# Odd planes of an inverse transform loaded in two parts, skipped columns, merged edge matmuls and one empty slot

## The chip, the cores and the metric

The kernel runs on one core of a Trainium2 chip. The metric is the device time of one execution in microseconds (us). The core has TensorE (PE: matmuls, and PEld: its weight loads), VectorE (DVE), ScalarE (ACT), GpSimd (POOL) and SyncE (SP), which here only issues DMAs. All DMAs run on the same 16 DMA engines. DRAM is the memory off the core, SBUF the memory on it (128 partitions), PSUM the buffer that matmuls write.

## The reference

For x of 2048 rows (s) and 1024 columns (d), with xn = layernorm(x) over d:

```python
X = rfft2(xn)                  # over s and d: 2048 x 513, complex
s = irfft2(X * (w_r + 1j * w_i))
h = silu(xn @ w1)              # w1: 1024 x 3584
g = silu(h @ w2)               # w2: 3584 x 1024
return x + s * g
```

Inputs and output are float32. Each float32 factor of a large product is split into a high and a low float16 part, and three matmuls (high by high, high by low, low by high) stand for one.

## The kernel before, in words

**Stages.** The kernel runs two lines of work side by side. The large one is the feed-forward part: xn @ w1 (mm1, line 491), then h @ w2 (mm2, line 580). The second product uses a scheme of seven products m (PRODUCTS, line 39), each with eight row blocks j. One (m, j) has two halves k of 21 matmuls, so there are 112 halves; half 2n + k is that of block n = 8m + j. The hidden layer lies in DRAM and comes back in ht tiles (load_h, line 558), two per block, from seven buffers; the w2 tiles are split into high and low by a generator (w2_gen, line 438) that takes one step per work call: it issues the load of a raw tile jr four steps ahead, and for products 4 and 5 a second load w, which GpSimd adds to jr (line 457) before ScalarE (high, line 284) and VectorE (low, line 287) split it.

The small line of work is the transform: a forward transform over d and s, a multiplication by the filter, and the inverse over s and then over d. Its matmuls stand between the halves of the large product.

**Planes.** f_gen (line 1029) makes the filtered spectrum in 16 steps u = 4q + j. The results of one q are four planes c of 1024 float16 columns in a high and a low part, stored to DRAM tiles zd[c] (lines 1099 to 1104). Planes 0 and 2 are one DMA per q. Planes 1 and 3 are two, one for each half r of the columns. edge_gen (line 1204) makes a correction for the first column of each group from nine small float32 matmuls (lines 1231 to 1233), which reverse the partition order with a permutation matrix.

**Inverse.** i_gen(c) (line 1324) handles one plane; the order is 1, 3, 0, 2 (IORDER). load_i(c) loads the plane into zt and its cosine table into kk, each in one buffer. For odd c it issues four DMAs of 512 KB, each to 64 partitions (first or second half r, row parity e), 8 KB in each partition, and then kk. edge_in (line 1315) copies the correction into zt. Then come four batches g: mat(g) is 24 matmuls of the inverse over s (line 1350 for odd c, 1358 for even), post(g) the butterflies on ScalarE and VectorE, split(g) the halves us for the next matmuls (lines 1428 and 1429). mat2(p), four times, is the inverse over d: 24 matmuls (line 1439) that read all four us tiles, and bfly(p) its butterflies.

**What sets the order.** Each engine runs its own instructions in the order in which the program issues them. The two lines of work are Python generators: after each half of mm2, tick() runs the issues that were deferred by a count of ticks (defer, line 203) and are due, and work() (line 1601) then takes steps of the transform's queue bg, at most three, until one yields PAUSE or until the planned clock of VectorE is more than LEAD = 1.0 us ahead of that of TensorE, and then one step of w2_gen. The planned clocks add costs by size (lines 241 to 252): 0.085 us + 1.045 ns per element and partition on VectorE, 0.4215 ns per column on TensorE; VectorE's clock is held at no more than 1 us behind TensorE's. switch() (line 1558) opens the pool of the inverse and calls load_i(1), and takes five more steps with PAUSE before i_gen(1) begins. close() runs all deferred issues. In this phase load_i(1) is called behind half 44, mat(0) of plane 1 behind half 50, and mat2(0) behind half 58; load_i(3) behind half 57.

Of the kernel before, what the change touches and what calls it, by code (L numbers as in the profile page):

```python
# [10 lines left out]
F16 = mybir.dt.float16  # L11
# [15 lines left out]
LEAD, PAUSE, LAST = 1.0, -1, 6  # L27
SECOND = 0.085, 1.045e-3
IORDER = (1, 3, 0, 2)
# [124 lines left out]
def spectral_ffn(ctx, tc, x, w_r, w_i, w1, w2, ca, kc, ci, tw, pm, out):  # L154
    nc = tc.nc
# [6 lines left out]
    ki = [kc[c][:, 1024:3088] for c in range(4)]  # L162
    wv = [t.rearrange("(m2 m1 q) k -> q m1 m2 k", m2=4, q=4) for t in (w_r, w_i)]

    dp = ctx.enter_context(tc.tile_pool(name="dram", bufs=1, space=DRAM))
# [8 lines left out]
    rd = [[dp.tile([256, 1024], F32, name=f"rd{side}_{j}") for j in range(4)] for side in range(2)]  # L174
    rows4 = [[t.rearrange("(a c) (q r k) -> a c q r k", c=4, q=4, r=2) for t in half] for half in rd]
    axis = [dp.tile([2, 4096], F32, name=f"axis{c}") for c in range(2)]
    zd = [dp.tile([128, 2, 4, 2, 512] if c % 2 else [128, 4, 2, 1024], F16, name=f"zd{c}") for c in range(4)]
    zpd = dp.tile([128, 4, 2, 4, 2], F16, name="zpd")
    SETS = ("sum_0", "sum_1", "sum_d"), ("one_0", "dif_1", "dif_0", "one_3")
    hds = {(k, g): dp.tile([128, 4 * len(m), NP, 2, 128], F16, name=f"hd_{k}_{g}") for k, m in enumerate(SETS) for g in range(2)}  # L180
# [14 lines left out]
    zps = cp.tile([128, 2, 4, 4, 2], F16, name="zps")  # L195
# [7 lines left out]
    def defer(n, fn):  # L203
        deferred.append([n, fn])
# [351 lines left out]
    part, ht = {}, {}  # L556
# [472 lines left out]
    def f_gen():  # L1029
# [64 lines left out]
        def low_z(u):  # L1094
            q, j = u // 4, u % 4
            zq, zsl = zqs[q], slice(16 * j, 16 * j + 16)
            nc.vector.scalar_tensor_tensor(zq[:, 1, :, zsl], zs_.pop(u), zs, zq[:, 0, :, zsl], op0=OP.mult, op1=OP.subtract)
            if j == 3:
                zv = zq.rearrange("m h (c n) i -> m h c (n i)", c=4)
                for c in range(0, 4, 2):  # L1100
                    defer(1, lambda c=c: nc.sync.dma_start(zd[c][:, q], zv[:, :, c]))
                for c in range(1, 4, 2):
                    for r in range(2):
                        defer(1, lambda c=c, r=r: nc.sync.dma_start(zd[c][:, r, q], zv[:, :, c, 512 * r:512 * r + 512]))  # L1104

        load_w(0)
        high_v(0)
# [9 lines left out]
        for u in range(16):  # L1117
            q, j = u // 4, u % 4
# [65 lines left out]
            for eng, lo_, hi_, pos in ((nc.vector, 0, 4, slice(0, 8, 2)), (nc.vector, 5, 8, slice(7, 1, -2)), (nc.gpsimd, 4, 5, slice(1, 2))):  # L1184
                ls = slice(lo_, hi_)
# [18 lines left out]
    def edge_gen():  # L1204

        g = nc.gpsimd
        xv = xsv
        room, perm = (tile_of(H["p"], [128, 512], F32, name, "pt", 6) for name in ("edge", "perm"))
        perm = perm[:, 0:384].rearrange("m (n k) -> m n k", n=3)
# [17 lines left out]
            g.tensor_copy(r0[:, n, 1:4], xv[:, n, 0, 3:0:-1])  # L1227
        yield 1
        ps = pf.tile([128, 512], F32, name="eps", tag="ff")
        for n in range(3):  # L1230
            nc.tensor.matmul(ps[:, n * 32 + 8:n * 32 + 32], perm[:, 0], rv[:, n, 1:4].rearrange("m q a r -> m (q a r)"), start=True, stop=True)
            nc.tensor.matmul(ps[:, n * 32:n * 32 + 8], perm[:, 1], rv[:, n, 0].rearrange("m a r -> m (a r)"), start=True, stop=False)
            nc.tensor.matmul(ps[:, n * 32:n * 32 + 8], perm[:, 2], r0[:, n].rearrange("m a r -> m (a r)"), start=False, stop=True)
        yield 1
        rr = piece(96).rearrange("m (n a r) -> m n a r", n=3, a=16)
        nc.scalar.activation(rr.rearrange("m n a r -> m (n a r)"), ps[:, 0:96], AF.Copy)
# [54 lines left out]
    C = {}  # L1291
# [8 lines left out]

    def load_i(c):
        zt = C["p"].tile([128, 8192], F16, name=f"zt{c}", tag="zt", bufs=1)
        if c % 2:
            src = zd[c].rearrange("(m e) r q h x -> r m e (q h) x", e=2)
            dst = zt.rearrange("m (e k x) -> m e k x", e=2, k=8)
            for r in range(2):
                for e in range(2):
                    nc.sync.dma_start(dst[64 * r:64 * r + 64, e], src[r, :, e])
        else:
            nc.sync.dma_start(zt.rearrange("m (q h x) -> m q h x", q=4, h=2), zd[c])  # L1310
        k = C["p"].tile([128, 2064], F16, name=f"kk{c}", tag="kk", bufs=1)
        nc.sync.dma_start(k, ki[c])
        C["z"][c], C["k"][c] = zt, k

    def edge_in(c):
        zt = C["z"][c]
        if c % 2:
            zt = zt.rearrange("m (e q h l i) -> m e q h l i", e=2, q=4, h=2, l=8)
            (nc.vector if c == IORDER[0] else nc.gpsimd).tensor_copy(zt[:, :, :, :, 0, 0], zps[:, :, c])
        else:  # L1320
            zt = zt.rearrange("m (q h r l i) -> m q h r l i", q=4, h=2, r=2, l=8)
            nc.gpsimd.tensor_copy(zt[:, :, :, :, 0, 0], zp[:, c].rearrange("m r q h -> m q h r"))

    def i_gen(c):
# [4 lines left out]
        yield PAUSE  # L1329
        zt, k = C["z"].pop(c), C["k"].pop(c)  # L1330
        if c % 2:
            zt = zt.rearrange("m (e q h l i) -> m e q h l i", e=2, q=4, h=2, l=8)
            k = k.rearrange("m (h y) -> m h y", h=2)[:, :, 0:1024].rearrange("m h (e q x) -> m e q h x", e=2, q=4)
        else:
            zt = zt.rearrange("m (q h r l i) -> m q h r l i", q=4, h=2, r=2, l=8)
            k = k.rearrange("m (h q r x) -> m q h r x", h=2, q=4, r=2)
# [3 lines left out]
        def mat(g):  # L1340
            ps = pt.tile([128, 1024], F32, name=f"iu{c}_{g}", tag="ft")
            psu[g] = ps
            ls = slice(2 * g, 2 * g + 2)
            if c % 2:
                for e in range(2):
                    for q in range(4):
                        o = ps[:, 512 * e + 128 * q:512 * e + 128 * q + 128]
                        for n, (zh, kh) in passes:
                            lhs = zt[:, e, q, zh, ls].rearrange("m l i -> m (l i)")
                            nc.tensor.matmul(o, lhs, k[:, e, q, kh], start=(n == 0), stop=(n == 2))  # L1350
                return
            width, second = (129, 127) if c else (128, 128)
            for q in range(4):
                for r, first in enumerate((0, second)):
                    o = ps[:, 256 * q + first:256 * q + first + width]
                    for n, (zh, kh) in passes:
                        lhs = zt[:, q, zh, r, ls].rearrange("m l i -> m (l i)")
                        nc.tensor.matmul(  # L1358
                            o, lhs, k[:, q, kh, r, 0:width], start=(r == 0 and n == 0), stop=(r == 1 and n == 2), skip_group_check=True)
# [74 lines left out]
        def mat2(p):  # L1434
            ps = pt.tile([128, 4, 256], F32, name=f"id{c}_{p}", tag="ft")
            for g in range(4):
                for r, cols in enumerate((slice(0, 130), slice(0 if g == 0 else 127, 256))):
                    for n, (uh, ch) in passes:
                        nc.tensor.matmul(  # L1439
                            ps[:, g, cols], us[g][:, uh, 4 * r + p], C["ci"][:, ch, g, r, cols],  # L1440
                            start=(r == 0 and n == 0), stop=(r == 1 and n == 2), skip_group_check=True)
            psd[p] = ps
# [59 lines left out]
        for i in range(6):  # L1502
            if i < 2:
                mat(i)
            if 1 <= i <= 4:
                post(i - 1)
            if i >= 2:
                split(i - 2)
            if c == IORDER[0] and i == 1:
                nc.sync.dma_start(C["ci"], ci)  # L1510
            yield PAUSE if i <= 3 else 3.9
            if 1 <= i <= 2:
                mat(i + 1)
        if c != IORDER[-1]:
# [283 lines left out]
```

## Time and profile before

| | before |
|---|---|
| median of 3 runs | 1208.4 us (1207.18 to 1208.95) |
| profiled execution | 1207.29 us, span 1205.5 us |
| PE busy | 1195.1 us (99%), 6600 matmuls |
| PEld busy | 597.1 us (50%) |
| DVE busy | 1009.7 us (84%) |
| ACT busy | 511.6 us (42%) |
| POOL busy | 210.2 us (17%) |
| DMA | 302.24 MB, mean 251 GB/s |
| granted TensorE clock | 0.999 of full speed |

The span is the time from the first to the last instruction. Busy times are of the profiled execution; a busy TensorE is not one at its peak, as matmuls are pipelined and their ends are modelled. A line number of a matmul group is that of the kernel before.

### The profile page before, as it was taken

How to read it: one execution, taken by the hardware profiler on the slowest of the kernel's cores; microseconds unless marked ns; L12 is line 12 of the kernel's file. 1: busy time of each engine (PE TensorE's matmuls, PEld its weight loads, DVE VectorE, ACT ScalarE, POOL GpSimd, SP SyncE). 2: the span in 40 equal slices, each digit the busy share in tenths (PEclk: the TensorE clock that was granted, in tenths of full speed). 3: DMA queues.
4: the chain of work that ended last, by engine and by line, in shares of the span. 5: the costliest groups of instructions: out<-in, count | busy, mean ns of one | idle time of the engine just before them, and what ended most of it. 6: DMA issues, size and time to landing. Idle time of an engine off the chain costs nothing.

```text
span 1205.5 us, 18361 instructions
## 1 busy us (share of the span) xinstructions
PE 1195.1 (99%) x6600; PEld 597.1 (50%) x6600; DVE 1009.7 (84%) x1971; ACT 511.6 (42%) x698; POOL 210.2 (17%) x297
## 2 busy tenths in 40 slices
PE   8999999999999999999999999999999999999998
PEld 5544445444544544444444444445455545555555
DVE  7778986996799598669968999999279898998696
ACT  7775654366466463445524233132032222343212
POOL 2330041102402300411100111125031231100000
PEclk9999999999999999999999999999999999999999
DMA  8788698589989976889989999993997989989577
GB/s 263 182 192 213 199 268 242 173 248 281 294 251 278 275 227 197 195 197 205 183 234 246 284 239 261 237 305 131 261 333 219 367 308 329 363 319 343 175 242 267
DMA packets 279540, 302.24 MB, mean 251 GB/s; under 512 B 47956, under 2 KB 206932, under 8 KB 278548
## 3 DMA queue, kind: packets, MB, share of 16 engines
q1 hardware_dynamic: 275848, 291.69, 81.1%
q0 software_dynamic: 3312, 9.24, 4.5%
q8 instruction: 52, 0.85, 0.3%
q14 instruction: 40, 0.33, 0.1%
q10 hardware_dynamic: 288, 0.13, 0.0%
HBM read 183.94 MB, written 110.77 MB: 244 GB/s over the span
## 4 chain that ended last, share of the span: by engine, by line
PE 93%; DVE 3%; DMA 3%; issue 1%; SPq 1%; ACT 0%; POOL 0%; ACTq 0%; DVEq 0%
PE pa L500 48%; PE pb L584 12%; PE pb L585 12%; PE pb L586 12%; PE id L1439 2%; PE fx L1070 2%; DMA ht<-hd 2%; PE iu L1358 1%; PE iu L1350 1%; PE fa L837 1%; PE fa L838 1%; PE fa L839 1%; DMA w<-in_B_w_dram 0%; DVE Z L1192 0%; SPq L1104 0%
## 5 line engine op out<-in xcount | busy, mean ns | idle before, releaser
L500 PE MATMUL pa<-xnT,w 128*128 128x512 f16 x2688 | 584.0, 379 | 0.0
L500 PEld LDWEIGHTS <-w 128*128 128x128 f16 x2688 | 261.6, 98 | 311.9 <-issue 0.3
L584 PE MATMUL pb<-w,ht 128*128 128x512 f16 (+2 forms) x812 | 300.4, 372 | 1.0 <-DMA ht<-hd 1.0
L585 PE MATMUL pb<-w,ht 128*128 128x512 f16 (+2 forms) x812 | 300.4, 372 | 0.0
L586 PE MATMUL pb<-w,ht 128*128 128x512 f16 (+2 forms) x812 | 300.3, 372 | 0.0
L509 ACT ACTIVATE h<-pa,s 128x512 f32<-128x512 f32 x112 | 75.9, 681 | 153.4 <-PE pa L500 112.8
L586 PEld LDWEIGHTS <-ht 128*128 128x128 f16 x812 | 79.5, 98 | 91.0
L584 PEld LDWEIGHTS <-ht 128*128 128x128 f16 x812 | 79.5, 98 | 87.7 <-DMA ht<-hd 1.1
L585 PEld LDWEIGHTS <-ht 128*128 128x128 f16 x812 | 79.5, 98 | 86.5
L284 ACT ACTIVATE w<-jr,sc 128x512 f16<-128x512 f32 x98 | 67.5, 712 | 64.6 <-POOL jr L457 60.4
L287 DVE SCALAR_TENSOR_TENSOR hoone<-h,hs,hoone 128x2048 f16<-128x2048 f32 x28 | 65.6, 2342 | 17.0 <-ACT hoone L284 17.0
L287 DVE SCALAR_TENSOR_TENSOR w<-jr,sc,w 128x512 f16<-128x512 f32 x98 | 78.0, 803 | 0.0
L1192 POOL TENSOR_TENSOR Z<-yb 128x32 f32<-128x32 f32 x64 | 34.9, 573 | 224.9 <-DVE yb L1169 224.9
L284 ACT ACTIVATE hoone<-h,hs 128x2048 f16<-128x2048 f32 x28 | 55.9, 1997 | 18.4 <-DMA hd<-hoone 18.4
L457 POOL TENSOR_TENSOR jr<-jr,w 128x512 f32<-128x512 f32 x28 | 38.8, 1387 | 123.8 <-DMA w<-in_B_w_dram 75.9
L1092 ACT ACTIVATE zq<-Z,zs 128x1024 f16<-128x1024 f32 x16 | 18.4, 1148 | 91.5 <-DVE Z L1192 54.3
L287 DVE SCALAR_TENSOR_TENSOR hosum<-hr,hs,hosum 128x1536 f16<-128x1536 f32 x28 | 50.7, 1811 | 7.2 <-ACT hosum L284 7.2
L284 ACT ACTIVATE hosum<-hr,hs 128x1536 f16<-128x1536 f32 x28 | 43.9, 1569 | 20.5 <-DMA hd<-hosum 12.1
L539 DVE TENSOR_TENSOR hr<-h 128x1024 f32<-128x1024 f32 x28 | 34.1, 1218 | 18.3 <-ACT h L509 18.0
L678 ACT ACTIVATE pl<-pl,c 128x512 f32<-128x512 f32 (+2 forms) x28 | 17.4, 655 | 72.7 <-DVE pl L654 42.4
L284 ACT ACTIVATE w<-w1r,rs 128x1024 f16<-128x1024 f32 x28 | 32.0, 1143 | 27.8 <-DVE w L287 23.5
L1192 DVE TENSOR_TENSOR Z<-yb 128x128 f32<-128x128 f32 (+1 forms) x128 | 42.3, 398 | 0.0
(246 smaller groups left out, 1520.4 us busy)
## 6 DMA issues: line engine op xcount, KB each, us to landing
ht<-hd SPq DMA_DIRECT2D x112, 448.0 KB, 6.5
hd<-hoone SPq DMA_DIRECT2D x28, 1024.0 KB, 8.6
hd<-hosum SPq DMA_DIRECT2D x28, 768.0 KB, 5.5
w1r<-in_B_w_dram SPq DMA_DIRECT2D x28, 512.0 KB, 6.6
w2m<-in_B_w_dram SPq DMA_DIRECT2D x28, 512.0 KB, 6.4
jr<-in_B_w_dram SPq DMA_DIRECT2D x56, 256.0 KB, 6.2
ws<-wd SPq DMA_DIRECT2D x42, 256.0 KB, 4.4
jr<-ws SPq DMA_DIRECT2D x42, 256.0 KB, 6.2
```

The source lines that it names most:

```text
L284: nc.scalar.activation(hi, raw, AF.Copy, scale=scale)
L287: nc.vector.scalar_tensor_tensor(lo, raw, scale, hi, op0=OP.mult, op1=OP.subtract)
L457: nc.gpsimd.tensor_tensor(raw[n], raw[n], more.pop(n), op=OP.add)
L500: nc.tensor.matmul(ps, w[:, wh, d], xt[:, xh, d], start=(n == 0), stop=(n == 23))
L509: nc.scalar.activation(hq[:, 2 * (c % 2) + f % 2], ps, AF.Silu, scale=s1[:, f:f + 1])
L539: tt(sums[:, 0:2], hq[:, 0::2], hq[:, 1::2], op=OP.subtract)
L584: nc.tensor.matmul(ps, hh[:, 0], w[:, 0], start=first, stop=False)
L585: nc.tensor.matmul(ps, hh[:, 0], w[:, 1], start=False, stop=False)
L586: nc.tensor.matmul(ps, hh[:, 1], w[:, 0], start=False, stop=last)
L1070: nc.tensor.matmul(o, k[:, c, kh], v[:, c, vh], start=(n == 0), stop=(n == 2))
L1192: eng.tensor_tensor(Z[:, ns, pos], x0[:, :, ls], x1[:, :, ls], op=o_)
L1439: nc.tensor.matmul(ps[:, g, cols], us[g][:, uh, 4 * r + p], C["ci"][:, ch, g, r, cols], start=(r == 0 and n == 0), stop=(r == 1 and n == 2 ...
```

## The change

The rows of planes 1 and 3 in DRAM get another order: zd[c] has a dimension b of two column groups of 256 in each half r. The stores go by high and low part h rather than by r. load_i for odd planes issues kk first, then four DMAs with b = 0 (256 KB each, 4 KB in each partition), and defers four DMAs with b = 1 by two ticks. Batches 0 and 1 of mat read the part b = 0, batches 2 and 3 the part b = 1; edge_in writes into part b = 0 only.

In mat2 the column spans of the first of the two row sets shrink from 130 to 129 for groups 1 to 3, and for group 0 one of the three passes of the second set covers columns 127 to 256 in place of all 256. The nine edge matmuls become three, each over all three n. i_gen(1) yields PAUSE once more behind the step i = 2.

```diff
-    zd = [dp.tile([128, 2, 4, 2, 512] if c % 2 else [128, 4, 2, 1024], F16, name=f"zd{c}") for c in range(4)]
+    zd = [dp.tile([128, 2, 2, 4, 2, 256] if c % 2 else [128, 4, 2, 1024], F16, name=f"zd{c}") for c in range(4)]
...
                 for c in range(1, 4, 2):
-                    for r in range(2):
-                        defer(1, lambda c=c, r=r: nc.sync.dma_start(zd[c][:, r, q], zv[:, :, c, 512 * r:512 * r + 512]))
+                    for h in range(2):
+                        defer(1, lambda c=c, h=h: nc.sync.dma_start(
+                            zd[c][:, :, :, q, h].rearrange("m r b x -> m (r b) x"), zv[:, h, c].rearrange("m (k x) -> m k x", k=4)))
...
-        for n in range(3):
-            nc.tensor.matmul(ps[:, n * 32 + 8:n * 32 + 32], perm[:, 0], rv[:, n, 1:4].rearrange("m q a r -> m (q a r)"), start=True, stop=True)
-            nc.tensor.matmul(ps[:, n * 32:n * 32 + 8], perm[:, 1], rv[:, n, 0].rearrange("m a r -> m (a r)"), start=True, stop=False)
-            nc.tensor.matmul(ps[:, n * 32:n * 32 + 8], perm[:, 2], r0[:, n].rearrange("m a r -> m (a r)"), start=False, stop=True)
+        p3 = ps[:, 0:96].rearrange("m (n x) -> m n x", n=3)
+        r3 = rv.rearrange("m n q a r -> m n (q a r)")
+        nc.tensor.matmul(p3[:, :, 8:32], perm[:, 0], r3[:, :, 8:32], start=True, stop=True)
+        nc.tensor.matmul(p3[:, :, 0:8], perm[:, 1], r3[:, :, 0:8], start=True, stop=False)
+        nc.tensor.matmul(p3[:, :, 0:8], perm[:, 2], r0.rearrange("m n a r -> m n (a r)"), start=False, stop=True)
...
         zt = C["p"].tile([128, 8192], F16, name=f"zt{c}", tag="zt", bufs=1)
+        k = C["p"].tile([128, 2064], F16, name=f"kk{c}", tag="kk", bufs=1)
         if c % 2:
-            src = zd[c].rearrange("(m e) r q h x -> r m e (q h) x", e=2)
-            dst = zt.rearrange("m (e k x) -> m e k x", e=2, k=8)
-            for r in range(2):
-                for e in range(2):
-                    nc.sync.dma_start(dst[64 * r:64 * r + 64, e], src[r, :, e])
+            nc.sync.dma_start(k, ki[c])
+            src = zd[c].rearrange("(m e) r b q h x -> r m e b (q h x)", e=2)
+            dst = zt.rearrange("m (e b x) -> m e b x", e=2, b=2)
+
+            def part(b):
+                for r in range(2):
+                    for e in range(2):
+                        nc.sync.dma_start(dst[64 * r:64 * r + 64, e, b], src[r, :, e, b])
+
+            part(0)
+            defer(2, lambda: part(1))
         else:
             nc.sync.dma_start(zt.rearrange("m (q h x) -> m q h x", q=4, h=2), zd[c])
-        k = C["p"].tile([128, 2064], F16, name=f"kk{c}", tag="kk", bufs=1)
-        nc.sync.dma_start(k, ki[c])
+            nc.sync.dma_start(k, ki[c])
...
         if c % 2:
-            zt = zt.rearrange("m (e q h l i) -> m e q h l i", e=2, q=4, h=2, l=8)
-            (nc.vector if c == IORDER[0] else nc.gpsimd).tensor_copy(zt[:, :, :, :, 0, 0], zps[:, :, c])
+            zt = zt.rearrange("m (e b q h l i) -> m e b q h l i", e=2, b=2, q=4, h=2, l=4)
+            (nc.vector if c == IORDER[0] else nc.gpsimd).tensor_copy(zt[:, :, 0, :, :, 0, 0], zps[:, :, c])
...
-                            lhs = zt[:, e, q, zh, ls].rearrange("m l i -> m (l i)")
+                            lhs = zt[:, e, g // 2, q, zh, slice(2 * (g % 2), 2 * (g % 2) + 2)].rearrange("m l i -> m (l i)")
...
-                for r, cols in enumerate((slice(0, 130), slice(0 if g == 0 else 127, 256))):
+                for r, span in enumerate((slice(0, 129 if g else 130), slice(127 if g else 0, 256))):
                     for n, (uh, ch) in passes:
+                        cols = slice(127, 256) if r and ch else span
...
             yield PAUSE if i <= 3 else 3.9
+            if c == IORDER[0] and i in (2,):
+                yield PAUSE
```

## Rows read from the trace of the kernel before

**Rows 1.** Busy time by stretch: us, busy by engine, PEclk, DMA share, GB/s.
```profile
850.00:900.00 50.00, 48.49 (x296) 24.75 (x294) 20.09 (x44) 9.81 (x15) 10.77 (x8) 1.00 0.96 308
```
**Rows 2.** Timeline of PE, 875 to 879: start, us, engine, line, operation [idle before <-releaser].
```profile
875.33 0.38 PE L586 MATMUL pb<-w,ht 128*128 128x512 f16 x1
876.26 1.50 PE L1350 MATMUL iu<-kk,zt 128*128 128x128 f16 x24 [0.55 <-DMA kk<-in_kc_dram]
878.71 0.39 PE L584 MATMUL pb<-w,ht 128*128 128x512 f16 x1 [0.96 <-DMA ht<-hd]
```
**Rows 3.** Timeline of SP: DMA issues at 74 and from 843 to 878.
```profile
74.32 0.60 SPq L533 DMA_DIRECT2D hd<-hosum  x1
...
846.01 5.02 SPq L1104 DMA_DIRECT2D zd<-zq  x4
...
858.11 2.94 SPq L1308 DMA_DIRECT2D zt<-zd  x4
...
865.55 2.58 SPq L560 DMA_DIRECT2D ht<-hd  x2
...
872.77 0.33 SPq L452 DMA_DIRECT2D w<-in_B_w_dram  x1
```
**Rows 4.** Timeline of PE: the first two groups of the inverse over d.
```profile
919.00 1.79 PE L1439 MATMUL id<-cis,us 128*128 128x130 f16 x24
...
926.69 1.69 PE L1439 MATMUL id<-cis,us 128*128 128x130 f16 x24
```
**Rows 5.** Timeline of DVE, 883 to 921.
```profile
883.99 0.69 DVE L1366 TENSOR_TENSOR ub<-iu,uc 128x512 f32<-128x512 f32 x1 [2.40 <-ACT uc L1364]
...
885.19 1.30 DVE L1377 TENSOR_TENSOR up<-ub 128x256 f32<-128x256 f32 x1
...
919.13 1.21 DVE L1429 SCALAR_TENSOR_TENSOR us<-uu,us 128x1024 f16<-128x1024 f32 x1
```
**Rows 6.** Busy time by stretch: after the length PE, PEld, DVE, ACT, POOL.
```profile
884.00:920.00 36.00, 36.00 (x224) 18.61 (x222) 35.72 (x77) 12.24 (x18) 11.36 (x8) 1.00 0.72 254
```
**Rows 7.** Timelines of POOL and ACT, 881 to 884.
```profile
881.38 1.34 POOL L457 TENSOR_TENSOR jr<-jr,w 128x512 f32<-128x512 f32 x1 [2.41 <-DMA w<-in_B_w_dram]
...
882.75 0.72 ACT L284 ACTIVATE w<-jr,sc 128x512 f16<-128x512 f32 x1 [2.55 <-POOL jr L457]
883.38 0.58 ACT L1364 ACTIVATE uc<-iu 128x512 f32<-128x512 f32 x1
```
**Rows 8.** Timeline of PE: first edge matmul, and the product behind the nine.
```profile
814.70 0.30 PE L1231 MATMUL eps<-edge,perm 128*128 128x24 f32 x2
...
816.62 0.38 PE L584 MATMUL pb<-w,ht 128*128 128x512 f16 x1
```
**Rows 9.** Chain of waits: start, us, what; float32 passes of 128 columns.
```profile
13.64 2.28 PE tp L803 x16
```
**Rows 10.** Groups by line and form, line 1439 | busy us, mean ns | idle.
```profile
L1439 PE MATMUL id<-cis,us 128*128 128x130 f16 x192 | 21.5, 220 | 0.0
...
L1439 PE MATMUL id<-cis,us 128*128 128x129 f16 x144 | 16.1, 220 | 0.0
...
L1439 PE MATMUL id<-cis,us 128*128 128x256 f16 x48 | 7.9, 273 | 0.0
```
**Rows 11.** Busy time by stretch; the last two columns are DMA share, GB/s.
```profile
76.00:78.00 2.00, 2.00 (x11) 0.88 (x9) 1.91 (x2) 0.00 (x0) 1.81 (x2) 1.00 1.03 293
852.00:856.00 4.00, 4.00 (x20) 1.86 (x19) 0.69 (x1) 0.00 (x0) 0.00 (x0) 1.00 1.07 365
864.00:872.00 8.00, 8.00 (x39) 3.63 (x37) 0.00 (x0) 0.00 (x0) 0.00 (x0) 1.00 0.97 201
876.00:882.00 6.00, 4.79 (x40) 2.85 (x40) 1.69 (x3) 1.21 (x2) 1.89 (x2) 1.00 1.03 399
```
**Rows 12.** Timelines of DVE and PE at 1044 to 1046.
```profile
1044.41 0.68 DVE L1367 TENSOR_TENSOR ub<-iu,uc 128x512 f32<-128x512 f32 x1
...
1045.15 1.53 PE L1358 MATMUL iu<-kk,zt 128*128 128x128 f16 x24
```

More of the change, by code (lines that the diff above doesn't have):

```diff
@@ L1331, in i_gen @@
         if c % 2:
-            zt = zt.rearrange("m (e q h l i) -> m e q h l i", e=2, q=4, h=2, l=8)
+            zt = zt.rearrange("m (e b q h l i) -> m e b q h l i", e=2, b=2, q=4, h=2, l=4)
             k = k.rearrange("m (h y) -> m h y", h=2)[:, :, 0:1024].rearrange("m h (e q x) -> m e q h x", e=2, q=4)
```

## The prediction

> **What bounds the kernel now.** I read the busy time by stretch first, then TensorE's timeline, then each engine's timeline back from TensorE's late starts. Of the stretches between 50 and 1200 us one shows TensorE less than fully busy: 850 to 900, with 48.49 of 50 [rows 1]. So TensorE's own work sets the time, and what it loses sits in two places 2 us apart. At 876.26 the first matmuls of the inverse over s (line 1350) start 0.93 us after the matmul before them, where 0.22 is the usual step: 0.71 lost to the load of kk, which SP issues behind four loads of plane 1. At 878.71 the next product starts after 0.96 us idle, waiting for its ht tile [rows 2]. Both came late because they stand in the queue behind the 2 MB of that plane, issued from 858.11 on; the ht load was issued at 865.55 [rows 3].
>
> A busy TensorE does not yet mean that less work on it is less time. The reader should look at the first 24 matmuls of the inverse over d: they take 1.79 us at 919.00 and 1.69 at 926.69 [rows 4]. The 0.10 is a wait inside the group, for the last split of us (line 1429), which VectorE runs from 919.13 to 920.34 [rows 5]. VectorE is at that point the end of a long chain: from 883.99 to 920.34 it is busy 35.72 us of 36 [rows 5, 6]. And 883.99 is not set by TensorE either: line 1366 waits for ScalarE's copy at 883.38, which stands in ScalarE's queue behind the split of a w2 tile at 882.75; that waits for GpSimd's sum (881.38, 1.34 us), and the sum for the load of w that SP issued at 872.77 [rows 3, 7]. That load lands at the end of a stretch in which the DMA engines are full.
>
> So two chains meet at 920.3: TensorE's, and SP, DMA, GpSimd, ScalarE, VectorE's, and the second is 0.1 us the longer.
>
> **The change, part by part.**
>
> *Merged edge matmuls.* Nine matmuls (two passes each) run from 814.70 to 816.62, 0.213 us each [rows 8]. Three remain, three times as wide. Lower end: the same 0.213 each, 0.64 in all, as those of 24 and of 8 columns keep the same step. Upper end: f32 passes of 128 columns take 2.28/16 = 0.14 us [rows 9], six of them 0.85. I take 0.72, so TensorE gains 1.2 us (1.07 to 1.28). Nothing on VectorE's side moves with it.
>
> *Skipped columns.* Per group of 24 one pass goes from 256 to 129 columns: 273 - 220 = 53 ns [rows 10]. The nine passes that go from 130 to 129 keep their price: both forms show 220 ns. 16 groups make 0.84 us, 15 of them behind 920.3 make 0.79.
>
> *Stores of the odd planes.* The same 16 stores of 256 KB, in pieces of 512 bytes for 1 KB. Only the last four (846 to 851) lie ahead of a late load [rows 3]. Behind the store of line 533 at 74.32, whose pieces have 512 bytes, a stretch moves 293 GB/s at a DMA share of 1.03, 284 when full; the present stores move 365 at 1.07, 341 when full [rows 11]. 1.05 MB takes 3.7 us in place of 3.1: 0.6 us later for all that follows in the queue. From below: nothing, if it hides in the gaps that the tiny zps loads leave; from above, if a 512-byte piece costs as much as a piece of 1 KB, another 3.1 us. I take 0.4.
>
> *Loads of the odd planes in two parts.* kk goes first, then four pieces of 256 KB; four more follow two ticks later. open_i runs in the work call behind half 44 of the products (112 halves of 21 matmuls, 4.53 us each); two ticks on is half 46, behind that half's pair of ht loads, and ahead of the jr and w loads of half 47 (w at 872.77). A plane lands at 201 GB/s, 256 KB and 448 KB loads over all partitions at 399 [rows 11]. From 865.5, when the ht load ahead has landed (the next issue, at 865.55, waits for it) [rows 3]: kk 1.3 us, half a plane 5.2, and 0.4 from the stores give 872.4. TensorE gets there at 876.26 - 0.71 - 1.2 = 874.35, so the wait for kk goes, with 2 us to spare. The ht tile: behind jr and w (0.66 each) and its own 1.15, 874.9, against 874.35 + 1.34 = 875.7: the 0.96 goes too. The other half lands by 881.3, and the first reader is due at about 886. SP's eight issues for five cost it nothing that ends last: at full queue its issues wait for landings.
>
> The w load on which VectorE's chain hangs has the same bytes ahead of it as before: kk, both halves of the plane, jr, w, two ht, jr. It lands no earlier, but 0.4 later, and VectorE starts at 884.4.
>
> By the Trainium skill (SBUF — State Buffer, Door 1: The DMA port swizzle) a transfer over 64 partitions reaches half of the ports, about 218 GB/s; the trace agrees with 201, and by that rule smaller pieces are no faster. The same page (The DMA setup-cost knee) gives each DMA a fixed 2 us, which speaks against cutting; taken one after another, an estimate from that page, four more pieces would cost 8 us. The share of 0.97 to 1.03 shows no gaps between pieces.
>
> *The empty slot.* The third batch (mat(3), post(2), split(1)) moves one half later. With the planner's own costs (0.62 for a 512-wide VectorE operation, about 6 for a batch) its lead then is 3.7, and -0.2 at the next call, below LEAD, so the fourth batch stays where it was: the slot only fills a half that was empty. Without it mat(3) would reach its PSUM buffer before VectorE frees it. VectorE's instructions from 884 to 920 are the same in number and kind, in another order. Cost nothing; up to 1 us either way by which of them meet a GpSimd sum (line 1377, 256 elements, takes 1.30 us at 885.19, twice line 1366 with its 512) [rows 5].
>
> **The sum.** TensorE reaches the inverse over d 1.2 + 0.71 + 0.96 = 2.9 us earlier, at 916.1, and wants the last split at 917.4. VectorE has it at 920.34 + 0.4. TensorE waits 3.4 us: what it gained is idle there, and 0.4 is lost. Behind that point it saves 0.79. But at 1045.15 it starts line 1358 just as VectorE ends line 1367 (1044.41 + 0.68) [rows 12]; of the 0.79, 0.36 (7 groups) comes before it and may be lost once more. I keep half of that: -0.6. Sum: +0.4 - 0.6 = -0.2 us. The profiled execution took 1207.29 (its span of 1205.5 and 1.8 around it), near the lowest of the runs (1207.18 to 1208.95, median 1208.4); as the change is a difference, I put it on the median, 1208.2, and take 1208.0, since rival A pulls further than C. About 0.2% (2.4 us) is what a measurement can tell from no change.
>
> **The rivals.**
>
> A. VectorE's chain moves too, and TensorE keeps all: 2.9 + 0.84 + up to 0.1 = 3.8 us, 1204.6. It needs the w load 3.4 us earlier, or that much less on VectorE. For it: 256 KB pieces of the two halves of the partitions alternate with full-width loads, and a transfer over half of the partitions leaves room beside it; if both halves of the plane moved at 399, the 2.1 MB would take 5.3 us, not 10.4, more than enough. Against it: the pieces keep their partitions and their order, and the share was full at 201.
>
> B. On the other side: the small copy into zt (edge_in, on VectorE ahead of the chain) or mat(0) waits for the second part as well, because the wait is taken for the tile and not for the region. Then the change does not do what it says. The second part lands at about 881, so mat(0) starts 4.7 us later than now, and TensorE, then the later of the two, ends 4.7 - 0.1 - 0.8 = 3.8 us later: 1212. It decides from a landing after about 877. Against it: the copy reads and writes the first part only, and the spare slice of a w2 tile is loaded while other slices are in use.
>
> C. 512-byte stores cost as much per piece as 1 KB ones: VectorE's chain starts 3.1 us late, 3.1 - 0.6 = 2.5 us: 1210.9. Slower than before from 0.6 us extra on, which is the rate of [rows 11]; that is why the sign of the likeliest case is open.
>
> **How the numbers follow.** Likeliest case 0.62, with its own range 1206.5 to 1209.8 (stores 0 to 1, collisions 1 either way). A 0.23, B 0.05, C 0.10. Faster: A and 0.05 of the likeliest case, 0.28. Slower: B and a third of C, 0.08. Same: 0.64. The range must reach A: 1204.4 to 1210.4 leaves out B, half of C, and the ends.
>
> **What would show it.** Right: TensorE idle for about 3 us inside the first 24 matmuls of line 1439, released by VectorE's line 1429; no idle at the first line 1350 and the product behind it; VectorE's first line 1366 at about 884, busy through to 921. Edge matmuls within 0.64 to 0.85 us, and the form of 256 columns 32 times for 48. Wrong: that line 1366 at 881 or earlier (A), or the copy of edge_in at 880 or later (B), or the last four stores landing over 1 us later than 1 KB pieces would (C). The prediction as a whole fails if the first group of line 1439 runs without idle.

## The result, and the profile after

| | before | changed |
|---|---|---|
| median of 22 runs each | 1206.41 us (1204.96 to 1209.46) | 1208.83 us (1205.71 to 1215.66) |
| ratio | | 1.0023, 95% interval 1.0014 to 1.0032 |
| profiled execution | 1207.29 us, span 1205.5 | 1209.12 us, span 1207.3 |
| PE busy, matmuls | 1195.1 us, 6600 | 1194.9 us, 6588 |
| DVE busy | 1009.7 us | 1010.3 us |
| granted TensorE clock | 0.999 | 0.998 |

The change makes the kernel 0.23% slower, about 2.4 us, where 0.2 us faster was forecast. (Two of the ratios below leave out one disturbed run each, of 2118 and of 1365 us.)

The merged and skipped columns are about 2 us less work for TensorE, and waits are not in its busy time; that the busy time falls by only 0.2 us says already that some of its matmuls took longer than before.

TensorE's timeline of the changed kernel (start, us, engine, line, operation, in brackets the idle time before and what ended it) at the places of [rows 2, 4, 8]:

```profile
814.67 0.34 PE L1233 MATMUL eps<-edge,perm 128*128 128x72 f32 x2
...
815.26 0.38 PE L584 MATMUL pb<-w,ht 128*128 128x512 f16 x1
...
874.18 1.50 PE L1358 MATMUL iu<-kk,zt 128*128 128x128 f16 x24
875.52 0.38 PE L584 MATMUL pb<-w,ht 128*128 128x512 f16 x1
...
886.71 1.50 PE L1358 MATMUL iu<-kk,zt 128*128 128x128 f16 x24 [0.62 <-DVE ub L1375]
...
916.58 1.06 PE L1448 MATMUL id<-cis,us 128*128 128x130 f16 x14
917.81 0.52 PE L1448 MATMUL id<-cis,us 128*128 128x129 f16 x6 [0.17 <-DVE us L1437]
920.87 2.96 PE L1448 MATMUL id<-cis,us 128*128 128x129 f16 x28 [2.54 <-DVE us L1437]
923.62 0.63 PE L584 MATMUL pb<-w,ht 128*128 128x512 f16 x1
```

The merged edge matmuls take 0.59 us, the waits for kk and the ht tile are gone, the inverse over d is reached at 916.58 in place of 919.00, and the rest is idle: 0.62 us at 886.71, where the third batch of the inverse over s waits for VectorE's first adds, and 0.17 + 2.54 us for VectorE's splits of us. The last two lines hold what the prediction did not have: 28 matmuls of 129 to 256 columns take 2.75 us behind the long idle, and a matmul of 512 columns shows 0.63 us for the usual 0.38. Busy time by stretch says why (us, then busy and number for PE, PEld, DVE, ACT, POOL, then PEclk, DMA share, GB/s):

```profile
852.00:856.00 4.00, 4.00 (x20) 1.81 (x19) 0.41 (x1) 0.00 (x0) 0.00 (x0) 1.00 1.06 320
...
885.00:921.00 36.00, 32.67 (x203) 16.69 (x201) 35.45 (x78) 12.48 (x19) 11.61 (x8) 1.00 0.75 259
921.00:925.00 4.00, 4.00 (x32) 3.10 (x31) 3.86 (x7) 1.93 (x5) 1.27 (x1) 0.57 0.99 332
...
922.00:923.00 1.00, 1.00 (x12) 1.00 (x11) 0.93 (x3) 0.70 (x3) 0.56 (x1) 0.50 0.98 396
```

and the same four us of the kernel before:

```profile
921.00:925.00 4.00, 4.00 (x35) 2.44 (x34) 3.87 (x9) 1.82 (x5) 1.27 (x1) 1.00 1.08 289
```

The granted clock is 0.57 over these four us, at its lower level (0.50, 1.2 GHz) for most of them: 4 x 0.43 = 1.7 us lost, an estimate.

The other chain, on SP, POOL and DVE of the changed kernel ([rows 3, 5, 7] before):

```profile
858.62 0.38 SPq L1307 DMA_DIRECT2D kk<-in_kc_dram  x1
859.06 2.40 SPq L1314 DMA_DIRECT2D zt<-zd  x4
...
868.12 4.12 SPq L1314 DMA_DIRECT2D zt<-zd  x4
...
872.96 0.38 SPq L452 DMA_DIRECT2D w<-in_B_w_dram  x1
```
```profile
882.73 1.27 POOL L457 TENSOR_TENSOR jr<-jr,w 128x512 f32<-128x512 f32 x1 [8.45 <-DMA w<-in_B_w_dram]
```
```profile
885.27 0.69 DVE L1374 TENSOR_TENSOR ub<-iu,uc 128x512 f32<-128x512 f32 x1 [8.38 <-ACT uc L1372]
...
919.60 1.22 DVE L1437 SCALAR_TENSOR_TENSOR us<-uu,us 128x1024 f16<-128x1024 f32 x1
...
1046.68 0.68 DVE L1375 TENSOR_TENSOR ub<-iu,uc 128x512 f32<-128x512 f32 x1
```

The w load is issued 0.2 us later than before, GpSimd's sum starts 1.35 later, VectorE 1.28 later and its last split ends 0.48 later. At 1047 TensorE waits for line 1375, as [rows 12] let expect: 0.60 us behind its last matmul's step, 0.14 before.

So the two profiled executions differ by +0.48 (VectorE's chain) + 1.7 (clock) - 0.79 (columns behind this point) + 0.46 (the wait at 1047) = 1.85 us; the spans differ by 1.8.

### The profile page after: what moved, and what is told of

The parts are those of the page before. It is cut to its first block, busy times and chain, and to the rows that moved or that the text cites. A ratio compares the mean times of both kernels' runs of the same rounds, so it can differ in the third digit from the quotient of the medians.

```text
span 1207.3 us, 18350 instructions
## 1 busy us (share of the span) xinstructions
PE 1194.9 (99%) x6588; PEld 596.4 (49%) x6588; DVE 1010.3 (84%) x1971; ACT 512.9 (42%) x698; POOL 211.6 (18%) x297
## 4 chain that ended last, share of the span: by engine, by line
PE 91%; DVE 4%; DMA 3%; SPq 1%; issue 1%; ACT 0%; DVEq 0%; ACTq 0%
PE pa L500 48%; PE pb L585 12%; PE pb L584 12%; PE pb L586 12%; PE id L1448 2%; PE fx L1070 2%; DMA zt<-zd 2%; PE fa L837 1%; PE fa L838 1%; PE fa L839 1%; PE iu L1366 1%; DMA x<-in_A_x_dram 1%; DMA ht<-hd 1%; PE iu L1358 0%; DVE uu L1407 0%
```

## The experiments

Each kernel is timed side by side with the kernel before, on the same chip. A measured number such as 1.0009 is the ratio of its time to that of the kernel before, with its 95% interval in brackets; 0.001 is 1.2 us. Four questions: is the clock what costs, is VectorE's chain what costs, which edit delays that chain, and what would keep the gain.

### Is it the clock?

Matmuls in the place of the idle:

```diff
             for g in range(4):
+                if c == IORDER[0] and p == 0 and g == 3:
+                    for _ in range(22):
+                        nc.tensor.matmul(ps[:, 3], us[0][:, 0, 0], C["ci"][:, 0, 0, 0], start=True, stop=True)
```

> The changed kernel, with 22 matmuls of 256 columns (f16, result overwritten) put into the place of TensorE's idle time, ahead of the fourth group of the first product of the inverse over d. They add no work behind the wait: 22 x 0.109 = 2.4 us beside a wait of 2.54 us. Theory (the idle lowers TensorE's clock, and the slow 3.4 us behind it are the larger part of what the change lost): granted clock 1.00 through 916 to 926, the first product's group still ends near 921.3, the half behind it starts 1.2 to 1.6 us earlier than in the changed kernel, and the run is about 1.5 us faster than the changed kernel, that is +0.4 to +0.9 us against the kernel before. Rival (the loss is VectorE's later chain and DMA traffic, the clock is not what costs): the same time as the changed kernel, +2.0 to +2.4 us.

Measured: 1.0009 (0.9997 to 1.0020). TensorE's timeline of this kernel:

```profile
918.70 0.41 PE L1451 MATMUL id<-cis,us 128*128 128x129 f16 x4 [1.40 <-DVE us L1437]
918.94 2.57 PE L1447 MATMUL id<-cis,us 128*128 128x256 f16 x22
921.34 2.23 PE L1451 MATMUL id<-cis,us 128*128 128x129 f16 x29
```
```profile
921.00:925.00 4.00, 3.86 (x43) 2.80 (x42) 3.90 (x6) 1.92 (x5) 1.27 (x1) 1.00 0.95 325
```

The filler (line 1447) lies where the idle was, and the clock stays at 1.00. The ratio is a little above the range expected (+0.4 to +0.9 us; it is +1.1), and its interval overlaps that of the changed kernel. As the kernels of this pair had run on different chips, they were run once more side by side.

> The changed kernel, beside the one with matmuls in the place of its idle, on the same chip. Theory (its loss is about half the lower clock behind the idle, half VectorE's later chain): 1.0015 to 1.003 of the kernel before, a mean granted clock of 0.998 or lower in half of its runs or more (20 of 34 so far).

> The changed kernel with 22 matmuls of 256 columns in the place of the idle, ahead of the fourth group of the first product of the inverse over d. Theory: 0.8 to 1.8 us less than the changed kernel beside it, a mean granted clock of 0.998 or lower in no more than a quarter of the runs (1 of 12 so far), and still 0.5 to 1.5 us above the kernel before, which is VectorE's later chain. Rival (the first difference was chance): the same time as the changed kernel within 0.5 us, and the low clock as often.

Measured: changed 1.0029 (1.0016 to 1.0041), filler 1.0016 (1.0004 to 1.0027). Medians 1210.20 and 1208.97: 1.2 us. A mean granted clock of 0.998 or lower was found in 8 and in 5 of 12 runs, so the quarter that was expected with the filler was missed. Over all runs it is 29 of 46 for the changed kernel (21 of the first 34, not the 20 of the expectation), 6 of 24 with the filler and 16 of 153 for the kernel before beside the experiments. In the second filler's profile the clock fell elsewhere, behind a wait at 889. The mean clocks agree in size: 0.99837 against 0.99931 before is 0.00094 x 1207 = 1.1 us. So the clock is worth an estimated 1.1 to 1.7 us of the 2.4 to 3.5, and the filler keeps the rest. Neither pair shows this alone, as its intervals overlap (in the second 1.0016 to 1.0041 and 1.0004 to 1.0027); that two pairs and the clocks agree speaks for it.

The changed kernel itself a second time:

> The changed kernel once more, beside the three that follow on the same chip. All theories: 1.002 times the kernel before, with TensorE idle for about 2.5 us in the first product of the inverse over d and a granted clock near 0.5 for some 3.4 us behind it.

Measured: 1.0021 (1.0004 to 1.0037). Timeline and stretch:

```profile
920.92 0.52 PE L1448 MATMUL id<-cis,us 128*128 128x129 f16 x6 [0.99 <-DVE us L1437]
923.98 0.74 PE L1448 MATMUL id<-cis,us 128*128 128x129 f16 x9 [2.54 <-DVE us L1437]
```
```profile
924.00:928.00 4.00, 4.00 (x39) 2.75 (x40) 3.87 (x7) 1.93 (x5) 1.27 (x1) 1.00 1.01 318
```

The idle is here, longer than in the first execution; the low clock, expected with it, is not. VectorE began at 887.56, 2.3 us later than in the first. Both terms change from one execution to the next, so no single profile settles their size; the changed kernel's times spread over 10 us, those of the kernel before over 4.5.

The edge matmuls undone, to shorten the idle from TensorE's side (the nine matmuls of before put back into the changed kernel):

```diff
-        nc.tensor.matmul(p3[:, :, 8:32], perm[:, 0], r3[:, :, 8:32], start=True, stop=True)
+        for n in range(3):
+            nc.tensor.matmul(ps[:, n * 32 + 8:n * 32 + 32], perm[:, 0], rv[:, n, 1:4].rearrange("m q a r -> m (q a r)"), start=True, stop=True)
...
```

> The changed kernel with the nine edge matmuls of before: TensorE has 1.2 to 1.36 us more work ahead of the inverse over s. Theory (what TensorE gains ahead of the inverse over d is only idle there, and an idle as long as 2.5 us also brings the clock down, which one of 1.5 us did not): the idle shrinks from 2.5 to 1.0 to 1.4 us, VectorE's chain ends where it did (920.8 +- 0.7), the granted clock stays at 1.00 from 921 to 925, and the run with more work is faster than the changed kernel, by 1.2 to 1.7 us (1.0005 to 1.0012 of the kernel before). Rival (the loss lies in later DMA and VectorE's chain alone): the same time as the changed kernel. A third view (TensorE's work always counts): 1.2 us slower than the changed kernel.

Measured: 1.0030 (1.0018 to 1.0042), beside 1.0021 for the changed kernel. The theory failed here: it had 1.0005 to 1.0012 and a clock of 1.00, but 6 of 11 runs had the low clock, though in the profile, of the fastest run, the idle was only 1.08. A shorter idle did not keep the clock up. The intervals overlap too far to choose between the rival and the third view.

### Is it VectorE's chain?

ScalarE's copy uc stands behind the split of a w2 tile that waits for the late load. Leave one step of that preparation to the next half, and the copy stands ahead:

```diff
             if chunks[0] == 4:
-                slot(wq)
+                halves[0] += 1
+                if halves[0] not in (51,):
+                    slot(wq)
```

> The changed kernel with the step of the weight's preparation that follows half 50 left to half 51: ScalarE's copy of the first product of the inverse over s then stands ahead of the split that waits for the late load of w, and VectorE's split of the same tile stands behind the first batch. Theory (VectorE's chain from the late w load to the inverse over d is what turns TensorE's gain into idle, and costs the clock): VectorE's first add starts at 876 to 879 in place of 884 to 887.5, its last split of us ends 3 to 8 us earlier than 920.8, TensorE has no idle over 0.5 us between 880 and 930, the granted clock stays at 1.00, and the run takes 2.5 to 4 us less than the kernel before (0.9967 to 0.998). Rival (VectorE's work over the whole stretch to 1075 is the bound, whichever order it is in): the idle moves to the products behind, as when the product was put off by one slot, and the time stays within 1.2 us of the kernel before or above it.

Measured: 0.9987 (0.9975 to 0.9999). The changed kernel loses its whole deficit and 1.6 us more, which is less than the 2.5 to 4 us expected. No matmul is moved, and neither are the late load of w and its place in the queue; but as the preparation stays one step behind from there on, the loads and sums that follow come one half later too. POOL, DVE and PE of its profile, and one stretch:

```profile
885.57 1.26 POOL L457 TENSOR_TENSOR jr<-jr,w 128x512 f32<-128x512 f32 x1 [9.35 <-DMA w<-in_B_w_dram]
```
```profile
878.09 0.68 DVE L1374 TENSOR_TENSOR ub<-iu,uc 128x512 f32<-128x512 f32 x1
...
915.98 1.22 DVE L1437 SCALAR_TENSOR_TENSOR us<-uu,us 128x1024 f16<-128x1024 f32 x1
```
```profile
993.59 0.29 PE L1448 MATMUL id<-cis,us 128*128 128x129 f16 x2 [0.90 <-ACT us L1436]
994.85 3.25 PE L1448 MATMUL id<-cis,us 128*128 128x129 f16 x28 [0.97 <-DVE us L1437]
```
```profile
995.00:997.00 2.00, 2.00 (x20) 1.87 (x19) 1.97 (x4) 1.33 (x4) 0.00 (x0) 0.52 0.97 236
```

VectorE starts at 878.09, ahead of the sum at 885.57, and its chain ends 3.6 us earlier than in the changed kernel; TensorE doesn't wait at 917. It now waits 0.90 + 0.97 us at the same place of the next odd plane, and the clock falls there: that is where the rest of the gain goes.

The same step moved in the kernel before, in the changed kernel without the slot, and in it with one load:

> The kernel before with that one step left to half 51, nothing else. Theory (in the kernel before TensorE's own work and its waits for kk and ht set the time, VectorE's chain is just even with it): VectorE's chain ends earlier by 3 us or more, TensorE keeps its waits of 0.7 and 1 us, and the time falls by no more than 1 us (0.9992 to 1.0). Rival (VectorE's chain is what sets the time of the kernel before in most executions): 1.5 us or more below the kernel before.

> The changed kernel with that step left to half 51 and without the empty slot. Theory (the slot only covers the wait for a PSUM buffer that VectorE frees late; with VectorE early it is worth nothing): within 0.6 us of the changed kernel with that step moved and the slot kept. Rival (the slot is needed for its own sake): 1.5 us or more slower than that one, with TensorE waiting 2 us at the fourth batch of the inverse over s.

> The changed kernel with that step left to half 51 and the odd plane loaded at one go, with kk behind it as in the kernel before (merged matmuls, skipped columns and slot kept). Theory (the two parts are worth the waits for kk and the ht tile): waits of 1.5 to 3 us in TensorE at 875 to 880, and 1.5 to 3 us slower than the changed kernel with that step moved. Rival (the two parts only move the wait): the same time as that one.

Measured: 0.9993 (0.9983 to 1.0003), 0.9993 (0.9984 to 1.0001), 1.0005 (0.9994 to 1.0017). In the kernel before, the moved step is worth under 1 us (its chain ends 1.7 us earlier there, not the 3 expected). With VectorE early the slot is worth 0.0006 x 1206 = 0.7 us, within the noise, and the two parts 0.0018 x 1206 = 2.2 us, at the edge of it: the intervals of 0.9987 and 1.0005 just overlap. The waits for kk and ht that come back with one load are 1.4 us in its profile, a little under the 1.5 expected.

The slot taken out of the changed kernel itself (two lines, `if c == IORDER[0] and i in (2,): yield PAUSE`):

> The changed kernel without the empty slot: the third batch of the inverse over s is planned one half earlier, as in the kernel before. Theory (the slot costs nothing and saves TensorE a wait for its PSUM buffer): TensorE waits 2 to 4 us at the fourth batch of matmuls, in place of most of the 2.5 us at the inverse over d; VectorE's chain ends within 0.7 us of 920.8; if an idle of that length lowers the clock wherever it falls, the time is within 0.7 us of the changed kernel. Rival (the slot itself is what costs, because it moves VectorE's work so that it ends later): VectorE's last split at 920.3 or earlier and a time at or below the kernel before.

Measured: 1.0034 (1.0021 to 1.0047). Its waits:

```profile
PE iu L1358 <- DVE ub L1375: 3.3, 2, 2.0
...
PE id L1448 <- DVE us L1437: 2.0, 2, 1.2
```

Most of the idle moves to the third and fourth batch (1.3 and 2.0 us), as expected. VectorE's chain ends at 922.3, 0.8 later than expected, having begun 1.1 later than in the changed kernel, and the time is 1.3 us above that one with intervals that overlap. The kernel is not faster without the slot, so no cost of the slot is seen.

### Which edit delays the chain?

The layout alone in the kernel before (512-byte stores, eight loads issued at once); one load in the changed kernel (`part(0)`, `part(1)` at once, kk behind them); two parts alone in the kernel before; and the kernel before with the matmul edits alone, and with the columns alone:

```diff
-            defer(2, lambda: part(1))
+            part(1)
+            nc.sync.dma_start(k, ki[c])
```

> The kernel before with the new layout of the odd planes alone: stores in pieces of 512 bytes, the plane loaded by eight DMAs in place of four, one right behind the other and kk behind them as before; no merged matmuls, no skipped columns, no empty slot. Theory (the smaller pieces cost little): GpSimd's sum behind the load of w on which VectorE's chain hangs starts 0 to 0.8 us later than in the kernel before, VectorE's chain with it, the clock stays at 1.00, and the time is 0 to 1 us above the kernel before. Rival (512-byte stores cost as much per piece as 1 KB ones): that sum starts 2.5 to 3.5 us later and the time is 2.5 to 3 us above the kernel before.

> The changed kernel with the odd plane loaded at one go and kk behind it, as before; merged matmuls, skipped columns, layout and slot kept. Theory (loading in two parts is what makes the late load of w land later, by 1 to 2 us, and so VectorE's chain; TensorE's waits for kk and ht that it removes lie beside that chain anyway): GpSimd's sum behind that load starts 21 to 23.3 us after the first load of the plane is issued (two parts: 22.3 to 27.6, mean 24.4), TensorE waits 1.5 us or more for kk and ht, its idle at the inverse over d is 1.5 us or less, and the time is 1.5 to 3 us below the changed kernel: 0.9993 to 1.0007 of the kernel before. Rival (the two parts are worth the waits that they remove): 1 us or more slower than the changed kernel.

> The kernel before with the new layout, kk first and the odd plane loaded in two parts, without merged matmuls, skipped columns and slot. Theory (two parts delay VectorE's chain, and the two waits that they take from TensorE come back at the inverse over d): TensorE's waits at 875 to 880 go, GpSimd's sum behind the late load of w starts 22.3 to 27.6 us after kk is issued, TensorE waits 1 to 3 us at the fourth batch of the inverse over s or at the inverse over d, and the time is 1 to 2.5 us above the kernel before (1.001 to 1.002). Rival (the loss needs TensorE's other savings): within 0.6 us of the kernel before or below it.

> The kernel before with the merged edge matmuls and the skipped columns, loads and slots as before. Theory (TensorE saves 2 us of work, of which 1.3 us turn into idle at the inverse over d, because VectorE's chain is the later one there): VectorE's chain ends where it did (920.3 to 921.8), TensorE waits 1 to 2.5 us for its last split, and the time is between -0.8 and +0.5 us of the kernel before. Rival (what TensorE saves counts): 1.6 us or more below the kernel before.

> The kernel before, with the skipped columns of the inverse over d alone. Theory (16 passes of 256 columns become 129: 16 x 53 ns = 0.84 us of TensorE's own time, with a part of what lies ahead of 1046 lost to a wait there): 0.4 to 0.85 us less than the kernel before, no other stretch moved. Rival (the smaller passes bring nothing, as the wait for VectorE's split or the one at 1046 takes it all): 0.0 to -0.2 us.

Measured: layout 0.9997 (0.9985 to 1.0009), one load 1.0001 (0.9989 to 1.0013), two parts 1.0016 (1.0004 to 1.0028), matmuls 0.9997 (0.9987 to 1.0006), columns 0.9997 (0.9986 to 1.0007). GpSimd's sum behind the late load of w, with one load in the changed kernel and with two parts in the kernel before (loads issued from 859.72 and 858.94; the second profile is of that kernel's slowest run, 1213.89 us, median 1208.01):

```profile
881.30 1.30 POOL L457 TENSOR_TENSOR jr<-jr,w 128x512 f32<-128x512 f32 x1 [2.45 <-DMA w<-in_B_w_dram]
```
```profile
887.27 1.27 POOL L457 TENSOR_TENSOR jr<-jr,w 128x512 f32<-128x512 f32 x1 [9.52 <-DMA jr<-in_B_w_dram]
```

From the first issue of the plane's loads to this sum it takes 21.4 to 23.3 us, mean 22.3, in seven profiles with one load, and 22.3 to 28.3, mean 24.7, in twelve with two parts. Layout and stores have no part in it: with them and one load it is 22.5, 21.4 and 21.6 (the sum of the layout kernel, at 883.12, was later than expected only as its loads were issued 2.5 us later). Two parts alone reproduce the loss, and one load takes it away, though TensorE then waits for kk and the ht tile:

```profile
PE iu L1358 <- DMA kk<-in_kc_dram: 1.9, 1, 1.9
...
PE pb L584 <- DMA ht<-hd: 1.0, 1, 1.0
```

One load also puts kk behind the plane again; no run separates the place of kk from the split into parts. Matmul savings of 2 us without a later load bring nothing that can be told from zero, with 0.93 us idle at the inverse over d in that profile, 1.46 with the columns alone.

Two of these kernels also tell the two losses apart. Two parts alone cost 1.9 us (0.0016) with the low clock in 1 of 11 runs and a mean clock like that of the kernel before beside it (0.99936, 0.99923): there VectorE's later chain is the loss, and TensorE's waits in its profile name it:

```profile
PE iu L1357 <- DVE ub L1374: 4.0, 2, 2.1
```

Matmul savings alone had the low clock in 6 of 11 runs; by the means, 0.99836 against 0.99923, that is about 1 us, half of what was saved.

### What would keep the gain?

The second part later, behind the w load; and the first product of the inverse over d one half later, in the first odd plane (in the changed kernel) or in the second one (`IORDER[1]`, with the step above moved):

```diff
-            defer(2, lambda: part(1))
+            defer(4 if c == IORDER[0] else 2, lambda: part(1))
```
```diff
         yield PAUSE
+        if c == IORDER[0]:
+            yield PAUSE
         for p in range(5):
```

> The changed kernel, with the second part of plane 1 issued two ticks later, so that the load of w on which VectorE's chain hangs stands ahead of it in the queue. Theory (that load's place behind 2 MB of the plane is what holds VectorE's chain at 885, and with it the whole gain on TensorE): VectorE's first add of the inverse over s starts 4 to 8 us earlier than 885.3, the wait of 2.5 us in the first product of the inverse over d goes, the clock stays at 1.00, and the run takes 3 to 4 us less than the kernel before (about 0.997). It fails if the second part lands too late for the third batch of matmuls (due at 885.7): then TensorE waits there instead. Rival (VectorE's chain is held by something else, TensorE's or ScalarE's own order): VectorE starts within 1 us of 885.3 and the time stays at +2 us.

> The changed kernel with one more empty slot, ahead of the first product of the inverse over d of plane 1, so that TensorE does one half of the main products (4.53 us) in the place of its idle. Theory (TensorE is early there and waits for VectorE's last split; only the order is at fault): no idle over 0.5 us between 900 and 930, a granted clock of 1.00 throughout, the waits for kk and for the ht tile still absent, and 2.5 to 3.8 us less than the kernel before (0.997 to 0.998). Rival (VectorE's chain, once late, is late everywhere behind: each later product of the inverse waits in turn): the idle comes back within 100 us, at the next products of the inverse or their evictions, and the time stays within 1 us of the kernel before.

> The changed kernel with the step behind half 50 left to half 51 (VectorE's chain of the first odd plane is early), and one more empty slot ahead of the first product of the inverse over d of the second odd plane, where TensorE then waited 1.9 us. Theory (that wait is one of order only): no idle at 992 to 995, and 1 to 2 us less than without this slot, 0.9970 to 0.9980 of the kernel before. Rival (VectorE is busy without a pause from 940 to 1000, and a product that comes later starves it later): the idle comes back between 1010 and 1080, and the time is the same as without this slot or more.

Measured: 0.9997 (0.9987 to 1.0006), 1.0078 (1.0058 to 1.0098), 0.9974 (0.9964 to 0.9985). With the part later VectorE starts at 880.88, as expected, but the next load of w is late in its turn, TensorE waits at 887 and at 888 (for the second wait the profile names the part), and 1.5 us of idle are left at the inverse over d, as VectorE's chain ends only at 920.3:

```profile
889.41 2.53 POOL L457 TENSOR_TENSOR jr<-jr,w 128x512 f32<-128x512 f32 x2 [9.80 <-DMA w<-in_B_w_dram]
```
```profile
887.09 0.83 PE L1358 MATMUL iu<-kk,zt 128*128 128x128 f16 x12 [1.23 <-issue]
888.25 0.44 PE L1358 MATMUL iu<-kk,zt 128*128 128x128 f16 x5 [0.34 <-DMA zt<-zd]
```

The product put off in the first plane was the worst of all. No idle is left at 921, as the theory had it; the rival was right that waits come back behind it, though it had the time within 1 us of the kernel before and not 9 above. The waits, in the profile of its fastest run:

```profile
PE id L1448 <- DVE us L1437: 1.9, 2, 1.0
PE id L1448 <- ACT us L1436: 1.9, 1, 1.9
...
PE iu L1358 <- DVE ub L1375: 1.2, 1, 1.2
...
PE iu L1366 <- DVE ub L1375: 0.9, 1, 0.9
```

all between 966 and 1075. They fit a VectorE that gets its input later and so is late for the products behind; that reading was not tested by itself. With VectorE early the same edit at the second plane leaves TensorE one wait behind the first 30 us, 0.95 us for an ht tile ahead of 876.56, with the clock at 1.00 in all stretches from 860 to 1040. That kernel is 3.1 us faster than the one before, and so faster than both.

## Why the prediction was wrong

**What held.** Two chains meet at 920, and TensorE's gain turns into idle there, released by line 1437 (1429 before): 2.7 us for 3.4 forecast, with another 0.6 at 886.71, which the prediction did not have. Matmuls alone (0.9997) and the moved step (0.9987) show it by experiment. The edge matmuls take 0.59 us, just under the range. There is no wait for kk and ht in this execution, but six of the other twelve profiles with two parts show 0.5 to 1.6 us for ht. The stores move 320 GB/s at a share of 1.06, 302 when full, 1.05 MB in 3.5 us for 3.1 at [rows 11]: the 0.4 us was right, and layout alone costs nothing measurable, which rules out rival C. Rival B is out as well: the copy of edge_in runs at 872.09, before the second part, issued up to 872.2, is in. No cost of the slot was seen. The -0.6 for columns behind the meeting point came out as -0.79 + 0.46 = -0.3 in the profiled pair.

**What was luck.** The forecast time, 1208.0 us, is close to the 1208.83 measured, and the range holds it, but only because the base was high: 1208.4 was the median of three runs of the kernel before, and that of 22 runs is 1206.41. Against the right base the forecast would have been 1206.2.

**The step that failed** is the one on VectorE's chain: "The w load on which VectorE's chain hangs has the same bytes ahead of it as before ... It lands no earlier, but 0.4 later, and VectorE starts at 884.4." The bytes are the same; the time that they take is not. VectorE's first add starts on average at 886.1 in nine profiles with two parts (883.3 to 889.8) and at 884.1 in five with one load (883.1 to 885.7), none with the step moved: 2.0 us later, not 0.4. Its last split of us ends at 922.1 against 920.5 on average, 1.6 us later. The one execution that was read before showed 883.99 and nothing of that spread. It is the new order of the loads that delays, kk first and the parts apart: the same eight pieces issued at once, with kk behind them, give 21.4 to 22.5. Why the queue then takes longer for the same bytes is not settled; its share is 0.97 to 1.04 from 860 to 880 in every profile, in both orders.

**The term that was missing**: idle of TensorE was priced at its length, and the clock at nothing. The clock was low in 29 of 46 runs, 1.1 us on average by the mean clocks, 1.2 by the medians of the filler beside it. By the Trainium skill (TensorE: Matmul & The Clock Gate, HAM oscillation) a wait between groups of matmuls can bring the clock down, so that the next group starts slow; the trace agrees, 0.57 over the four us behind 2.54 us idle. The same page (Part 1) says that the slow start of a kernel varies from run to run; what is seen here behind a wait varies too, 0.57 and 1.00 behind the same 2.54 us. What decides when the clock falls is not shown: it is not the length of the idle alone, as the same 2.54 us had both.

With both, the sum about closes, as an estimate: 1.6 to 2.0 for VectorE's chain in place of 0.4, 1.1 for the clock, -0.3 for -0.6 give 2.4 to 2.8 us, for 2.4 measured (1.7 to 3.9 by the interval).

Rival A needed VectorE's chain to move too. It did not by itself; with one step moved and one product put off, 3.1 of the 3.8 us that it named came.

## What to carry to other kernels

Where two engines' chains meet within a few tenths of a us, work taken off one is worth nothing until the other moves, and one edit has either sign: two parts cost 2.7 us while VectorE was late (1.0023, 1.0001 without them, on different chips) and seem to have saved 2.2 us once it was early (0.9987, 1.0005 without them, at the edge of the noise). Look for what holds the later chain in an in-order queue, here a ready copy behind a split that waits for a load, before shortening the earlier one. Price an idle stretch of TensorE with the clock behind it, and take the start of a chain that hangs on a DMA from several executions.

## What was not expected of the hardware

The clock fell to 0.52 behind two waits of 0.90 and 0.97 us 0.3 us apart (the changed kernel with the step moved), and did not fall behind 0.99 and 2.54 us (the changed kernel, second profile). The sum that waits for a load of 256 KB at one place in a full queue came 22.3 to 28.3 us behind the first of the plane's loads with these in two parts, and 21.4 to 23.3 us behind it with the same bytes in one.
